# An attention and feed-forward kernel: where the units of one batch are scored, in which order a hand-written list puts them between the matmuls, and how the last block is cut

## The chip, the core and the metric

The kernel runs on one core of a Trainium2 chip. The metric is the device time of one execution in microseconds. A core has TensorE (matmuls), VectorE, ScalarE and GpSimd, which work side by side, each on its own queue in order, and a SyncE queue (SP) that only issues transfers. Engines wait for one another by semaphores.

## What is computed

Two steps follow each other. The first is attention over 8 batches of 576 positions with 8 heads of 64. Heads 0 to 3 see the 32 last positions ("plain"), heads 4 to 7 see every fourth of the last 128 ("dilated"). The second is a gated feed-forward block on the 4608 tokens of 512 values that the attention gives.

```python
def _attn_ref(q, k, v):
    B, H, S, D = q.shape                      # 8, 8, 576, 64
    scores = 1.0 / np.sqrt(D) * np.matmul(q, k.transpose(0, 1, 3, 2))
    rel = pos[:, None] - pos[None, :]
    mask_plain = (rel >= 0) & (rel < 32)
    mask_dil = (rel >= 0) & (rel < 128) & (rel % 4 == 0)
...
    attn = np.exp(scores - np.max(scores, axis=-1, keepdims=True))
    attn = attn / (np.sum(attn, axis=-1, keepdims=True) + 1e-09)
    return np.matmul(attn, v)

def _moe_ref(x, w_gate, w_val, w_out):        # x: 4608 x 512
    g = x @ w_gate                            # 512 x 1536
    gelu = 0.5 * g * (1.0 + erf(g * inv_sqrt2))
    return gelu * (x @ w_val) @ w_out         # 1536 x 512
```

## The kernel before, in words

**The feed-forward block** sets the frame. The tokens are cut into nine chunks of 512 (`run_chunk`, line 904). Each chunk c has two stages. In *gate stage* c, 96 matmuls of 128x512 (`ffn1_part`, line 636) make twelve blocks of the gate and of the value, four matmuls each; ScalarE applies the GELU to a gate block (`g0` to `g11`, line 801), VectorE multiplies with the value block (`u0` to `u11`, line 806). In *output stage* c, 48 matmuls of 128x512 (`ffn2`, line 643), twelve for each of four token blocks, multiply with w_out; ScalarE copies each block out of PSUM and SP stores it (`e0@c` to `e3@c`, `store`, lines 651 to 658). The store of the fourth block of a stage falls into the gate stage after it. The last token block of chunk 8 goes through `last_block` (line 660): its 512 columns are taken as two halves of twelve matmuls each, ScalarE copies the first (line 678) and SP stores it, VectorE copies the second (line 676) and ScalarE's queue stores it.

**The attention** is cut into 32 units of two heads of one batch: unit n is of batch n // 4. In batches 2 and 3 the dilated pairs come first, in the others the plain ones. A unit has these pieces, each a short word of the lists below:

- `Sn`: scores on TensorE (`two_s`, line 473); `Pn`: exponential on ScalarE (line 508); `Mn`: mask multiplied on VectorE (line 513).
- `Dn`: sums over the keys, on TensorE (`two_den`); `Nn`: products with v, on TensorE (`two_num`).
- the reciprocals of the sums, in one of two ways: `Tn` and `Bn` on VectorE (a transpose, line 597, a reciprocal, line 599, and a transpose back, line 614), or `An` on ScalarE (a logarithm, line 606, and an exponential, line 608).
- `Xn`: the product of both, written by VectorE into `xT` (line 627), the operand of the gate stages. `pair` (line 357) tells which of the four 128-row parts of `xT` a unit fills.

The number behind an @ is a place in PSUM: for S a bank (a unit takes two), for D and N 0 for banks 4 and 5, or 1 for banks 6 and 7. Two words with a plus between them are *joint*: their 64x64 matmuls are put into different quarters of TensorE's array alternately (`emit_tiles`, line 448, matmuls on line 457). A word alone is issued as 128x128 matmuls (`emit`, line 446).

**The loads.** `Fb` (`load_first`, line 291) loads q and k of batch b through SP into a staging tile, and GpSimd casts them to 16 bits (lines 221 and 233). `Hb` (`load_rest`, line 317) has SP turn them (four transposing transfers, line 273), loads v, and has GpSimd spread k into blocks for the scores (lines 289 and 281) and cast v (line 262). `R` is H3, F4 and H4. The staging tile, the 16-bit tile and the turned k (`dense`) are each there once, so a batch's loads wait for the casts and spreads of the batch before.

**The order** is written out by hand (`tc.manual_schedule()`, line 55). For each stage there is a list of words, `gates[c]` (line 829) or `outs[c]` (line 865), which `run_program` (line 782) takes one after the other: a number emits so many matmuls of the stage, any other word emits its piece at that place, each into the queue of its engine. `E` and `G` load ScalarE's function table for the attention and for the GELU. `firsts[c]` (line 893) gives the order of the first 16 matmuls of a gate stage as triples: block, gate or value, and the part of `xT` that is read, so that parts which come late are read late. The gate blocks use banks 0 to 3 in turn (`gate_banks`, line 753), the output blocks the pair of banks that `out_banks` (line 779) gives. Output stage c usually carries the four units of batch c + 1; their last N and X stand in the gate stage after it. Before the change, output stage 3 carries batch 4 and also S20, S21, P20, P21 and D20 of batch 5, whose loads F5 and H5 stand in gate stage 3.

Of the kernel before, what the change touches and what calls it, by code (L numbers as in the profile page):

```python
# [21 lines left out]
def kernel(  # L22
# [12 lines left out]
    NT, DM = out.shape  # L35
# [624 lines left out]
    def last_block(c, tb, bank):  # L660

        osb = osbp.tile([P, DM], F32, tag="osb")
        t0 = c * CH + tb * P
        for half in range(2):
            cs = slice(half * DM // 2, (half + 1) * DM // 2)
            for fc in range(NNB):
                nc.tensor.matmul(  # L667
                    ps[:, bank + 2 * half - 2, cs],
                    u_all[:, fc, tb * P : (tb + 1) * P],
                    wo_t[fc // 4][:, fc % 4, cs],  # L670
                    start=(fc == 0),
                    stop=(fc == NNB - 1),
                )
            src = ps[:, bank + 2 * half - 2, cs]
            if half:
                nc.vector.tensor_scalar(osb[:, cs], src, 1.0 / USCALE, None, ALU.mult)
            else:
                nc.scalar.activation(osb[:, cs], src, AF.Copy, bias=0.0, scale=1.0 / USCALE)
            (nc.scalar if half else nc.sync).dma_start(out=out[t0 : t0 + P, cs], in_=osb[:, cs])
# [102 lines left out]
    def run_program(c, words, mms, banks):  # L782
# [3 lines left out]
        for word in words.split():  # L786
# [10 lines left out]
            elif kind in units:  # L797
                units[kind](*args)
            elif kind == "g":
                g = ffn.tile([P, CH], F16, tag="g")  # L800
                nc.scalar.activation(g, ps[:, gate_banks(c, args[0])[0], :], AF.Gelu)  # L801
                tiles["g", args[0]] = g
            elif kind == "u":
                nb = args[0]
                val = ps[:, gate_banks(c, nb)[1], :]
                nc.vector.scalar_tensor_tensor(u_all[:, nb, :], tiles.pop(("g", nb)), USCALE, val, ALU.mult, ALU.mult)  # L806
            elif kind in "ew":
                at = args[1] if len(args) > 1 else c
                store(at, args[0], out_banks(at)[args[0]], "act" if kind == "e" else "dve")
            elif kind == "L":  # L810
                mms.clear()
                last_block(c, 3, banks[3])
            elif kind == "V":
                second_v() if args else second()
            elif kind == "F":
                load_first(args[0])
            elif kind == "H":
                load_rest(args[0])
            elif kind == "R":
                load_rest(3)  # L820
                load_first(4)
                load_rest(4)
            elif kind == "E":
                nc.scalar.preload_act_table_set("natural_log_exp_and_others")
            else:
                nc.scalar.preload_act_table_set("gelu_and_others")
# [7 lines left out]
            "t9@5@1 t11@7@0 5 g8 u8 8 g9 u9 8 g10 u10 1 t12@4@1 t14@6@0 t13@5@1 t15@7@0 7 g11 u11"  # L834
        ),
        1: (
            "4 N7@0 e3@0 F3 1 X7 1 G 8 g0 2 g1 1 u0 2 u1 2 g2 4 u2 4 g3 4 u3 4 g4 4 u4 4 g5 4 u5 4 g6 4 u6 4 g7 4 "
            "u7 4 g8 4 u8 4 g9 4 u9 4 g10 4 u10 4 g11 3"
        ),
        2: (  # L840
            "4 N11@0 e3@1 R 1 X11 G 7 g0 3 g1 u0 3 u1 3 g2 4 u2 4 g3 4 u3 4 g4 4 u4 4 g5 4 u5 4 g6 4 u6 4 g7 4 u7 "
            "4 g8 4 u8 4 g9 4 u9 4 g10 4 u10 4 g11 3"
        ),
        3: (
            "4 N15@0 e3@2 F5 H5 1 X15 G 7 g0 3 g1 u0 3 u1 3 g2 4 u2 4 g3 4 u3 4 g4 4 u4 4 g5 4 u5 4 g6 4 u6 4 g7 "
            "4 u7 4 g8 4 u8 4 g9 4 u9 4 g10 4 u10 4 g11 3"
        ),
        4: (
            "G 6 e3@3 F6 H6 T20 3 g0 2 N20@1+D21@0 u0 1 B20 1 g1 4 u1 3 X20 1 g2 4 u2 N21@1 1 T21 3 g3 3 B21 3 u3 "
            "2 g4 1 X21 4 u4 3 g5 4 u5 4 g6 4 u6 4 g7 4 u7 4 g8 4 u8 4 g9 4 u9 4 g10 4 u10 4 g11 3"  # L850
        ),
        5: (
            "G 5 B24 N24@1+D25@0 e3@4 F7 H7 g0 1 X24 4 u0 1 N25@1 T25 2 g1 3 B25 4 u1 1 g2 2 X25 3 u2 3 g3 4 u3 4 "
            "g4 4 u4 4 g5 4 u5 4 g6 4 u6 4 g7 4 u7 4 g8 4 u8 4 g9 4 u9 4 g10 4 u10 4 g11 3"
        ),
        6: (
            "G 2 T28 4 e3@5 1 N28@1+D29@0 B28 g0 2 u0 3 X28 1 g1 4 u1 N29@1 1 T29 3 g2 3 B29 3 u2 2 g3 1 X29 4 u3 "
            "3 g4 4 u4 4 g5 4 u5 4 g6 4 u6 4 g7 4 u7 4 g8 4 u8 4 g9 4 u9 4 g10 4 u10 4 g11 3"
        ),
        7: (  # L860
            "G 6 e3@6 2 g0 3 u0 2 g1 4 u1 4 g2 4 u2 4 g3 4 u3 4 g4 4 u4 4 g5 4 u5 4 g6 4 u6 4 g7 4 u7 4 g8 4 u8 4 "
# [2 lines left out]
    }  # L864
    outs = {
        0: (
            "V1 F2 S4@4+S5@6 1 E P4 10 P5 1 M4 S6@2+S7@6 M5 1 P6 2 D4@0 P7 1 M6 3 T4 2 e0@0 3 M7 1 e1@0 H2 2 B4 7 "
            "N4@1+D5@0 1 A5 X4 5 N5@0+D6@1 e2@0 1 A6 X5 5 N6@1+D7@0 1 A7 X6 1"
        ),
        1: (  # L870
            "1 u11 5 S8@0+S9@6 1 E P8 10 P9 M8 1 S10@0+S11@4 e0@1 M9 1 P10 2 D8@1 P11 1 M10 3 T8 e1@1 5 M11 "
            "N8@0+D9@1 B8 1 A9 3 X8 2 N9@1 e2@1 2 X9 2 D10@0 1 A10 5 N10@1+D11@0 1 A11 X10 1"
        ),
        2: (
            "1 u11 5 S12@2+S13@6 1 E P12 10 P13 M12 1 S14@2+S15@4 e0@2 M13 1 P14 2 D12@1 P15 1 M14 3 T12 e1@2 5 "
            "M15 N12@0+D13@1 B12 1 A13 3 X12 2 N13@1 e2@2 2 X13 2 D14@0 1 A14 5 N14@1+D15@0 1 A15 X14 1"
        ),
        3: (
            "1 u11 5 S16@0+S17@6 1 E P16 10 P17 1 M16 S18@0+S19@4 e0@3 M17 2 P18 1 D16@1 P19 1 M18 3 A16 M19 4 "
            "N16@0+D17@1 e1@3 S20@0 A17 X16 5 P20 N17@1+D18@0 1 A18 X17 1 S21@0 1 M20 2 P21 N18@0+D19@1 1 e2@3 "  # L880
            "X18 2 A19 4 M21 1 N19@1+D20@0 1 X19"
        ),
        4: (
            "1 u11 5 S22@2+S23@4 1 E P22 10 P23 M22 1 S24@2+S25@6 e0@4 M23 1 P24 2 D22@0 P25 1 M24 3 A22 1 M25 3 "
            "N22@1+D23@0 e1@4 1 X22 6 T23 1 e2@4 4 B23 N23@1+D24@0 1 X23 6 T24"
        ),
        5: (
            "1 u11 5 S26@0+S27@4 1 E P26 10 P27 M26 1 S28@0+S29@6 e0@5 M27 1 P28 2 D26@0 P29 1 M28 1 S30@0 A26 1 "
            "M29 3 N26@1+D27@0 P30 1 X26 1 e1@5 1 S31@0 1 P31 1 T27 5 M30 e2@5 N27@1+D28@0 B27 4 M31 4 X27 3"
        ),  # L890
        6: "D30@0 u11 1 E A30 5 N30@1+D31@0 1 T31 5 X30 N31@0 e0@6 4 B31 4 X31 5 e1@6 12 e2@6 11",
    }
    firsts = {
        0: "000 100 002 102 001 101 010 110 012 112 011 111 003 103 013 113",
        1: "000 001 010 011 002 012 100 101 102 110 111 112 003 013 103 113",
        2: "002 003 012 013 000 010 102 103 100 112 001 011 101 113 110 111",
        3: "002 003 012 013 000 010 102 103 100 112 001 011 101 113 110 111",
        4: "000 001 002 010 011 012 100 003 013 101 102 103 110 111 112 113",
        5: "000 001 002 003 010 011 012 013 100 101 102 103 110 111 112 113",
        6: "000 001 002 003 010 011 012 013 100 101 102 103 110 111 112 113",  # L900
        7: "000 001 002 003 010 011 012 013 100 101 102 103 110 111 112 113",
    }

# [38 lines left out]
```

## Time and profile before

| what | us |
|---|---|
| median of six runs | 335.56 |
| lowest and highest of them | 333.42, 337.39 |
| the profiled execution's own time | 337.39 |
| its span, first to last instruction | 335.7 |
| TensorE busy | 325.9 |
| VectorE busy | 159.3 |
| ScalarE busy | 157.6 |
| GpSimd busy | 149.9 |

The mean granted clock of TensorE is 0.995. The profiled execution is one of the six. Its span is what the profile's views divide; 1.7 us of its time lie outside. Starts of the stages in that execution, read off the order of the matmuls: gate stage 3 at 126, output stage 3 at 146.9, gate stage 4 at 166.3, output stage 4 at 188.2, gate stage 5 at 201.2, output stage 5 at 222.9. The last matmul ends at 332.45.

The profile has, beside busy times, the span in 40 slices (each 8.4 us, busy shares in tenths), a list of waits (who waited for whom, us in total, times, longest), the chain of work that ended last, and the instructions in order of time. A matmul of 512 columns shows a mean of 379 ns there since the matmuls are pipelined; from start to start it is 0.216 us. ACT stands for ScalarE, DVE for VectorE, PE for TensorE, PEld for its weight loads, POOL for GpSimd.

### The profile page before, as it was taken

Reading aid. Unit: us, or ns where it says so; the run is one execution under the profiler, and the core shown is the slowest. Engines: PE = TensorE matmul, PEld = TensorE weight load, DVE = VectorE, ACT = ScalarE, POOL = GpSimd, SP = SyncE. Lnnn points to the kernel's source line nnn. Section 1 sums busy time; section 2 is a strip of 40 time slices with the busy share of each in tenths; the row PEclk is TensorE's granted clock in tenths of the full one; section 3 lists DMA queues with packets and bytes.
Section 4 is the critical chain, followed back from the end, with each engine's and each line's share of the span. In section 5 each row is a group of like instructions: output and inputs, shape, how many; then the busy total and the mean of one; then the engine's idle time right before and its main releaser. Section 6 shows DMA issues by size and latency. Waiting matters only on the chain.

```text
span 335.7 us, 7368 instructions
## 1 busy us (share of the span) xinstructions
PE 325.9 (97%) x2959; PEld 160.9 (48%) x2959; DVE 159.3 (47%) x241; ACT 157.6 (47%) x236; POOL 149.9 (45%) x246
## 2 busy tenths in 40 slices
PE   7899999999999999996999999999999999999996
PEld 5744545444544454443544454445444544444443
DVE  6854654434643364432584478347743424303320
ACT  2763567436653566366733563357335343223321
POOL 8899777649437748444925841484000000000000
PEclk9999999999999999999899999999999999999999
DMA  8999986898798998999779636973100110020002
GB/s 185 195 195 180 197 171 148 231 175 213 172 265 184 195 231 159 252 199 173 192 181 240 158 113 151 245 174 94 62 2 1 65 62 0 2 94 31 0 33 94
DMA packets 109026, 47.97 MB, mean 143 GB/s; under 512 B 83648, under 2 KB 104512, under 8 KB 108992
## 3 DMA queue, kind: packets, MB, share of 16 engines
q1 hardware_dynamic: 97216, 39.99, 51.9%
q0 software_dynamic: 11216, 6.79, 14.2%
q10 hardware_dynamic: 560, 0.72, 0.8%
q8 instruction: 23, 0.38, 0.4%
q14 instruction: 11, 0.09, 0.1%
HBM read 37.75 MB, written 9.44 MB: 141 GB/s over the span
## 4 chain that ended last, share of the span: by engine, by line
PE 86%; DMA 7%; SPq 3%; POOL 1%; DVE 1%; issue 1%; ACT 0%; DVEq 0%; POOLq 0%
PE ps L636 52%; PE ps L643 26%; PE ps L457 4%; PE ps L446 3%; DMA dense<-s 2%; DMA wg<-in_moe_w_gate_dram 2%; DMA xT<-in_q_dram 2%; SPq L214 1%; DMA stage<-in_q_dram 1%; PE ps L667 1%; SPq L217 1%; POOL q L289 1%; PE ps L387 1%; POOL xT L176 0%; SPq L658 0%
## 5 line engine op out<-in xcount | busy, mean ns | idle before, releaser
L806 DVE SCALAR_TENSOR_TENSOR u_all<-g,ps 128x512 f16<-128x512 f16 x108 | 73.8, 687 | 104.7 <-PE ps L636 101.3
L801 ACT ACTIVATE g<-ps 128x512 f16<-128x512 f32 x108 | 64.1, 597 | 112.2 <-PE ps L636 112.2
L636 PE MATMUL ps<-xT,wg 128*128 128x512 f16 x432 | 113.8, 379 | 0.4 <-DMA wg<-in_moe_w_gate_dram 0.2
L636 PE MATMUL ps<-xT,wv 128*128 128x512 f16 x432 | 112.8, 379 | 0.0
L643 PE MATMUL ps<-wo,u_all 128*128 128x512 f16 x420 | 100.1, 382 | 0.0
L636 PEld LDWEIGHTS <-wv 128*128 128x128 f16 x432 | 42.2, 98 | 50.0
L636 PEld LDWEIGHTS <-wg 128*128 128x128 f16 x432 | 42.0, 98 | 49.9 <-issue 0.8
L643 PEld LDWEIGHTS <-u_all 128*128 128x128 f16 x420 | 37.9, 98 | 40.8 <-issue 0.3
L262 POOL CAST v<-stage 64x576 f16<-64x576 f32 x60 | 43.4, 723 | 6.5 <-DMA stage<-in_v_dram 3.4
L627 DVE TENSOR_TENSOR xT<-ps,rb 128x576 f16<-128x576 f32 x32 | 29.9, 937 | 22.2 <-PE ps L457 16.1
L221 POOL CAST s<-stage 128x640 f16<-128x640 f32 x24 | 17.1, 741 | 38.4 <-DMA stage<-in_q_dram 24.8
L508 ACT ACTIVATE P<-ps 128x832 f16<-128x832 f32 (+1 forms) x32 | 25.5, 834 | 15.6 <-PE ps L457 10.6
L654 ACT ACTIVATE osb<-ps 128x512 f32<-128x512 f32 x34 | 20.2, 595 | 26.0 <-PE ps L643 25.7
L289 POOL COPY q<-dense 64x1152 f16<-64x1152 f16 (+1 forms) x28 | 20.2, 720 | 15.5 <-DMA dense<-s 11.9
L281 POOL COPY q<-dense 64x512 f16<-64x512 f16 x28 | 16.4, 612 | 6.7 <-DMA dense<-s 3.7
L233 POOL CAST s<-stage 128x512 f16<-128x512 f32 x24 | 14.1, 617 | 10.1 <-DMA stage<-in_q_dram 5.2
L606 ACT ACTIVATE lg<-ps 128x576 f32<-128x576 f32 x18 | 11.7, 652 | 10.2 <-PE ps L457 6.8
L513 DVE TENSOR_TENSOR P<-P,two_d 128x768 f16<-128x768 f16 x14 | 10.1, 736 | 11.0 <-ACT P L508 10.7
L513 DVE TENSOR_TENSOR P<-P,two_p 128x832 f16<-128x832 f16 x14 | 10.1, 734 | 9.7 <-ACT P L508 9.6
L457 PEld LDWEIGHTS <-v 64*64 64x64 f16 x380 | 9.1, 110 | 8.5 <-issue 6.8
L608 ACT ACTIVATE rb<-lg 128x576 f32<-128x576 f32 x18 | 12.3, 683 | 0.6
L597 DVE STREAM_TRANSPOSE dt<-ps 128x576 f32<-128x576 f32 x14 | 10.8, 774 | 1.7 <-ACT rb L608 1.7
(81 smaller groups left out, 197.7 us busy)
## 6 DMA issues: line engine op xcount, KB each, us to landing
out_dram<-osb SPq DMA_DIRECT2D x35, 256.0 KB, 2.3
stage<-in_v_dram SPq DMA_DIRECT2D x32, 144.0 KB, 3.6
stage<-in_v_dram SPq DMA_DIRECT2D x28, 128.0 KB, 3.2
stage<-in_q_dram SPq DMA_DIRECT2D x24, 128.0 KB, 3.5
stage<-in_k_dram SPq DMA_DIRECT2D x24, 128.0 KB, 2.9
stage<-in_q_dram SPq DMA_DIRECT2D x6, 512.0 KB, 4.5
stage<-in_k_dram SPq DMA_DIRECT2D x6, 512.0 KB, 5.5
wg<-in_moe_w_gate_dram POOLq DMA_DIRECT2D x6, 256.0 KB, 6.8
```

The lines of the kernel that those rows point to most:

```text
L221: nc.gpsimd.tensor_copy(s16[:, 1280 * t + 640 * g : 1280 * t + 640 * g + 640].rearrange("p (k c) -> p k c", k=5), st_of(i).rearrange("p (k ...
L262: nc.gpsimd.tensor_copy(dst[half_of(x), at, half_of(x, g * swap)], st[half_of(x), at])
L289: nc.gpsimd.tensor_copy(out_, src[half].rearrange("p g (j c) -> p g j c", c=64))
L457: nc.tensor.matmul(o[cols], lhs[rows, cols], rhs[rows], start=st, stop=end, skip_group_check=True)
L508: nc.scalar.activation(pt[:, 0 : src.shape[1]], src, AF.Exp, bias=0.0, scale=scale)
L513: nc.vector.tensor_tensor(pt, pt, mask, ALU.mult)
L627: nc.vector.tensor_tensor(dst, num, rb, ALU.mult)
L636: nc.tensor.matmul(ps[:, bank, :], w[:, kc, ns], xT[kc][:, tok], start=first, stop=end)
L643: nc.tensor.matmul(ps[:, bank, :], u_all[:, fc, tb * P : (tb + 1) * P], wo_t[fc // 4][:, fc % 4, :], start=(fc == 0), stop=(fc == NNB - 1),)
L654: nc.scalar.activation(osb, ps[:, bank, :], AF.Copy, bias=0.0, scale=1.0 / USCALE)
L801: nc.scalar.activation(g, ps[:, gate_banks(c, args[0])[0], :], AF.Gelu)
L806: nc.vector.scalar_tensor_tensor(u_all[:, nb, :], tiles.pop(("g", nb)), USCALE, val, ALU.mult, ALU.mult)
```

## The change

Three things are altered. `last_block` cuts the last token block into 384 and 128 columns instead of 256 and 256. No unit of batch 5 is in output stage 3 any more; S20 and S21 are the first joint words of output stage 4, which now carries all of batch 5 and, as words alone, S24 and S25 of batch 6. And the lists of the stages 1 to 6 (in stage 0 one matmul's place at the end) are drawn anew: single words N9 and D10, and N13 and D14, become joint; the reciprocals of units 8, 12, 20, 21 and 23 are made by A instead of T and B; places in PSUM, the places of stores and of the units that are left over into a gate stage, and the orders in `firsts` are altered with them. The order of SP's and GpSimd's queues is the same but for the width of the last store.

```diff
--- before.py
+++ after.py
@@ -662,7 +662,7 @@
         osb = osbp.tile([P, DM], F32, tag="osb")
         t0 = c * CH + tb * P
         for half in range(2):
-            cs = slice(half * DM // 2, (half + 1) * DM // 2)
+            cs = slice(384 * half, 384 + 128 * half)
             for fc in range(NNB):
                 nc.tensor.matmul(
                     ps[:, bank + 2 * half - 2, cs],
@@ -834,28 +834,29 @@
             "t9@5@1 t11@7@0 5 g8 u8 8 g9 u9 8 g10 u10 1 t12@4@1 t14@6@0 t13@5@1 t15@7@0 7 g11 u11"
         ),
         1: (
-            "4 N7@0 e3@0 F3 1 X7 1 G 8 g0 2 g1 1 u0 2 u1 2 g2 4 u2 4 g3 4 u3 4 g4 4 u4 4 g5 4 u5 4 g6 4 u6 4 g7 4 "
+            "5 N7@0 e3@0 F3 1 X7 1 G 7 g0 2 g1 1 u0 2 u1 2 g2 4 u2 4 g3 4 u3 4 g4 4 u4 4 g5 4 u5 4 g6 4 u6 4 g7 4 "
             "u7 4 g8 4 u8 4 g9 4 u9 4 g10 4 u10 4 g11 3"
         ),
         2: (
-            "4 N11@0 e3@1 R 1 X11 G 7 g0 3 g1 u0 3 u1 3 g2 4 u2 4 g3 4 u3 4 g4 4 u4 4 g5 4 u5 4 g6 4 u6 4 g7 4 u7 "
+            "5 N11@1 e3@1 R 1 X11 G 7 g0 3 g1 u0 3 u1 2 g2 4 u2 4 g3 4 u3 4 g4 4 u4 4 g5 4 u5 4 g6 4 u6 4 g7 4 u7 "
             "4 g8 4 u8 4 g9 4 u9 4 g10 4 u10 4 g11 3"
         ),
         3: (
-            "4 N15@0 e3@2 F5 H5 1 X15 G 7 g0 3 g1 u0 3 u1 3 g2 4 u2 4 g3 4 u3 4 g4 4 u4 4 g5 4 u5 4 g6 4 u6 4 g7 "
+            "5 N15@0 e3@2 F5 H5 1 X15 G 7 g0 3 g1 u0 3 u1 2 g2 4 u2 4 g3 4 u3 4 g4 4 u4 4 g5 4 u5 4 g6 4 u6 4 g7 "
             "4 u7 4 g8 4 u8 4 g9 4 u9 4 g10 4 u10 4 g11 3"
         ),
         4: (
-            "G 6 e3@3 F6 H6 T20 3 g0 2 N20@1+D21@0 u0 1 B20 1 g1 4 u1 3 X20 1 g2 4 u2 N21@1 1 T21 3 g3 3 B21 3 u3 "
-            "2 g4 1 X21 4 u4 3 g5 4 u5 4 g6 4 u6 4 g7 4 u7 4 g8 4 u8 4 g9 4 u9 4 g10 4 u10 4 g11 3"
+            "2 N19@1 e3@3 F6 H6 1 X19 1 G 8 g0 3 g1 u0 3 u1 3 g2 4 u2 4 g3 4 u3 4 g4 4 u4 4 g5 4 u5 4 g6 4 u6 4 "
+            "g7 4 u7 4 g8 4 u8 4 g9 4 u9 4 g10 4 u10 4 g11 3"
         ),
         5: (
-            "G 5 B24 N24@1+D25@0 e3@4 F7 H7 g0 1 X24 4 u0 1 N25@1 T25 2 g1 3 B25 4 u1 1 g2 2 X25 3 u2 3 g3 4 u3 4 "
-            "g4 4 u4 4 g5 4 u5 4 g6 4 u6 4 g7 4 u7 4 g8 4 u8 4 g9 4 u9 4 g10 4 u10 4 g11 3"
+            "G 2 N23@1+D24@0 1 e3@4 F7 H7 X23 6 T24 3 g0 2 N24@1+D25@0 g1 u0 1 B24 4 u1 2 g2 1 X24 3 u2 2 N25@1 "
+            "T25 2 g3 3 B25 3 u3 2 g4 1 X25 4 u4 3 g5 4 u5 4 g6 4 u6 4 g7 4 u7 4 g8 4 u8 4 g9 4 u9 4 g10 4 u10 4 "
+            "g11 3"
         ),
         6: (
-            "G 2 T28 4 e3@5 1 N28@1+D29@0 B28 g0 2 u0 3 X28 1 g1 4 u1 N29@1 1 T29 3 g2 3 B29 3 u2 2 g3 1 X29 4 u3 "
-            "3 g4 4 u4 4 g5 4 u5 4 g6 4 u6 4 g7 4 u7 4 g8 4 u8 4 g9 4 u9 4 g10 4 u10 4 g11 3"
+            "G 4 T28 2 e3@5 2 g0 2 N28@1+D29@0 u0 1 B28 2 g1 2 T29 5 u1 N29@0 g2 1 X28 3 B29 4 u2 1 g3 2 X29 4 u3 "
+            "2 g4 4 u4 4 g5 4 u5 4 g6 4 u6 4 g7 4 u7 4 g8 4 u8 4 g9 4 u9 4 g10 4 u10 4 g11 3"
         ),
         7: (
             "G 6 e3@6 2 g0 3 u0 2 g1 4 u1 4 g2 4 u2 4 g3 4 u3 4 g4 4 u4 4 g5 4 u5 4 g6 4 u6 4 g7 4 u7 4 g8 4 u8 4 "
@@ -864,40 +865,40 @@
     }
     outs = {
         0: (
-            "V1 F2 S4@4+S5@6 1 E P4 10 P5 1 M4 S6@2+S7@6 M5 1 P6 2 D4@0 P7 1 M6 3 T4 2 e0@0 3 M7 1 e1@0 H2 2 B4 7 "
-            "N4@1+D5@0 1 A5 X4 5 N5@0+D6@1 e2@0 1 A6 X5 5 N6@1+D7@0 1 A7 X6 1"
+            "V1 F2 S4@4+S5@6 1 E P4 10 P5 1 M4 S6@2+S7@6 M5 1 P6 2 D4@0 P7 1 M6 3 T4 2 e0@0 3 M7 1 e1@0 H2 2 B4 8 "
+            "N4@1+D5@0 1 A5 X4 5 N5@0+D6@1 e2@0 1 A6 X5 5 N6@1+D7@0 1 A7 X6"
         ),
         1: (
-            "1 u11 5 S8@0+S9@6 1 E P8 10 P9 M8 1 S10@0+S11@4 e0@1 M9 1 P10 2 D8@1 P11 1 M10 3 T8 e1@1 5 M11 "
-            "N8@0+D9@1 B8 1 A9 3 X8 2 N9@1 e2@1 2 X9 2 D10@0 1 A10 5 N10@1+D11@0 1 A11 X10 1"
+            "1 u11 5 S8@0+S9@6 1 E P8 10 P9 M8 1 S10@0+S11@4 e0@1 M9 1 P10 2 D8@1 P11 1 M10 3 A8 1 M11 3 "
+            "N8@0+D9@1 e1@1 1 A9 X8 7 e2@1 1 N9@1+D10@0 1 A10 X9 8 N10@0+D11@1 1 A11 X10"
         ),
         2: (
-            "1 u11 5 S12@2+S13@6 1 E P12 10 P13 M12 1 S14@2+S15@4 e0@2 M13 1 P14 2 D12@1 P15 1 M14 3 T12 e1@2 5 "
-            "M15 N12@0+D13@1 B12 1 A13 3 X12 2 N13@1 e2@2 2 X13 2 D14@0 1 A14 5 N14@1+D15@0 1 A15 X14 1"
+            "1 u11 5 S12@2+S13@4 1 E P12 10 P13 M12 1 S14@2+S15@6 e0@2 M13 1 P14 2 D12@0 P15 1 M14 3 A12 1 M15 3 "
+            "N12@1+D13@0 e1@2 1 A13 X12 7 e2@2 1 N13@0+D14@1 1 A14 X13 8 N14@1+D15@0 1 A15 X14"
         ),
         3: (
-            "1 u11 5 S16@0+S17@6 1 E P16 10 P17 1 M16 S18@0+S19@4 e0@3 M17 2 P18 1 D16@1 P19 1 M18 3 A16 M19 4 "
-            "N16@0+D17@1 e1@3 S20@0 A17 X16 5 P20 N17@1+D18@0 1 A18 X17 1 S21@0 1 M20 2 P21 N18@0+D19@1 1 e2@3 "
-            "X18 2 A19 4 M21 1 N19@1+D20@0 1 X19"
+            "1 u11 5 S16@0+S17@6 1 E P16 10 P17 1 M16 1 S18@0+S19@4 e0@3 M17 1 P18 1 D16@1 1 P19 1 M18 2 A16 1 "
+            "M19 4 N16@0+D17@1 e1@3 1 A17 X16 6 e2@3 N17@1+D18@0 1 A18 X17 6 N18@0+D19@1 1 A19 X18 3"
         ),
         4: (
-            "1 u11 5 S22@2+S23@4 1 E P22 10 P23 M22 1 S24@2+S25@6 e0@4 M23 1 P24 2 D22@0 P25 1 M24 3 A22 1 M25 3 "
-            "N22@1+D23@0 e1@4 1 X22 6 T23 1 e2@4 4 B23 N23@1+D24@0 1 X23 6 T24"
+            "1 u11 5 S20@2+S21@4 1 E P20 10 P21 1 M20 1 S22@2+S23@6 e0@4 M21 1 P22 1 D20@0 1 P23 1 M22 2 A20 "
+            "S24@2 M23 3 N20@1+D21@0 e1@4 P24 1 X20 3 A21 1 M24 S25@2 1 N21@1+D22@0 P25 1 X21 1 A22 3 M25 2 "
+            "N22@0+D23@1 e2@4 1 A23 X22 6"
         ),
         5: (
-            "1 u11 5 S26@0+S27@4 1 E P26 10 P27 M26 1 S28@0+S29@6 e0@5 M27 1 P28 2 D26@0 P29 1 M28 1 S30@0 A26 1 "
-            "M29 3 N26@1+D27@0 P30 1 X26 1 e1@5 1 S31@0 1 P31 1 T27 5 M30 e2@5 N27@1+D28@0 B27 4 M31 4 X27 3"
-        ),
-        6: "D30@0 u11 1 E A30 5 N30@1+D31@0 1 T31 5 X30 N31@0 e0@6 4 B31 4 X31 5 e1@6 12 e2@6 11",
+            "1 u11 5 S26@0+S27@4 1 E P26 10 P27 M26 2 S28@0+S29@6 e0@5 M27 1 P28 1 D26@0 1 P29 1 M28 1 S30@0 A26 "
+            "1 M29 4 N26@1+D27@0 P30 1 e1@5 X26 2 S31@0 1 P31 1 T27 3 e2@5 2 M30 1 N27@1+D28@0 B27 3 M31 4 X27 1"
+        ),
+        6: "D30@1 u11 1 E A30 6 N30@0+D31@1 1 T31 5 X30 e0@6 1 N31@1 3 B31 4 X31 4 e1@6 12 e2@6 11",
     }
     firsts = {
         0: "000 100 002 102 001 101 010 110 012 112 011 111 003 103 013 113",
-        1: "000 001 010 011 002 012 100 101 102 110 111 112 003 013 103 113",
-        2: "002 003 012 013 000 010 102 103 100 112 001 011 101 113 110 111",
-        3: "002 003 012 013 000 010 102 103 100 112 001 011 101 113 110 111",
-        4: "000 001 002 010 011 012 100 003 013 101 102 103 110 111 112 113",
-        5: "000 001 002 003 010 011 012 013 100 101 102 103 110 111 112 113",
-        6: "000 001 002 003 010 011 012 013 100 101 102 103 110 111 112 113",
+        1: "000 001 010 011 100 002 012 101 102 110 111 112 003 013 103 113",
+        2: "002 003 012 013 102 000 010 103 100 112 113 001 011 101 110 111",
+        3: "002 003 012 013 102 000 010 103 100 112 113 001 011 101 110 111",
+        4: "000 001 002 010 011 012 100 101 102 110 003 013 103 111 112 113",
+        5: "000 001 002 010 011 012 100 101 102 110 003 013 103 111 112 113",
+        6: "000 001 002 010 011 003 012 013 100 101 102 103 110 111 112 113",
         7: "000 001 002 003 010 011 012 013 100 101 102 103 110 111 112 113",
     }
```

## The prediction

> **What bounds the kernel now.** First the page: the row of busy times, and the two rows of the span in 40 slices that show TensorE and its clock.
>
> ```profile
> PE 325.9 (97%) x2959; PEld 160.9 (48%) x2959; DVE 159.3 (47%) x241; ACT 157.6 (47%) x236; POOL 149.9 (45%) x246
> PE   7899999999999999996999999999999999999996
> PEclk9999999999999999999899999999999999999999
> ```
>
> TensorE sets the time; the others are under half. After the start only one slice of 8.4 us is open, the 19th (151 to 159 us: a 6), and the clock dips once, one slice later (an 8). Next the list of waits: of TensorE's own, only one is long.
>
> ```profile
> PEld L446 <- POOL q L289: 2.9, 1, 2.9
> PE ps L446 <- POOL q L289: 2.7, 1, 2.7
> ```
>
> The line 446 emits one unit alone, the line 289 is GpSimd's spread of the plain k blocks. The chain that ended last shows what came before it:
>
> ```profile
> 143.95 4.12 DMA stage<-in_q_dram
> 148.07 7.50 DMA dense<-s
> 155.70 1.15 POOL q L289
> 156.90 1.16 POOL q L289
> 158.10 0.54 PE ps L446 x9
> 158.64 1.58 PE ps L643 x5
> ```
>
> At 158.10 TensorE starts S20, the first scores of batch 5. It had been empty since 155.33 (2.75 us); it waited for a transfer that turns batch 5's k and for the spread behind it. Behind the stall five 128x512 matmuls take 1.58 us where a few stages on twelve take 2.70. So I asked for busy time and clock in half-microsecond stretches (the columns: us, TensorE, its weight loads, VectorE, ScalarE, GpSimd, clock, DMA share, GB/s):
>
> ```profile
> 158.50:159.00 0.50, 0.50 (x7) 0.26 (x5) 0.00 (x0) 0.32 (x1) 0.08 (x1) 1.00 0.14 37
> 159.00:159.50 0.50, 0.50 (x3) 0.16 (x2) 0.00 (x0) 0.50 (x1) 0.50 (x2) 0.58 0.75 223
> 162.00:162.50 0.50, 0.50 (x10) 0.50 (x8) 0.50 (x1) 0.48 (x1) 0.50 (x2) 0.51 0.79 178
> 162.50:163.00 0.50, 0.50 (x7) 0.22 (x4) 0.09 (x1) 0.28 (x1) 0.50 (x1) 1.00 0.88 202
> ```
>
> Between these rows the clock stands at 0.50 throughout, from about 159.1 to 162.5: 3.4 us at half speed, a loss of 1.7 us. The stall thus costs 2.75 + 1.7 = 4.45 us. A cross-check: output stage 3 lasts 146.9 to 166.3 = 19.4 us; its parts (48 matmuls at 0.216, two joint S at 0.59, four joint N and D at 0.6, three single units at 0.34) make 15.0. The rest is 4.4.
>
> **The change part by part.**
>
> *S20 and S21 leave output stage 3.* The only wait on GpSimd goes: -2.75 us. Does the clock loss go with it? The row: idle 2.75 us, then 3.4 us at 0.50. The rule: the Trainium skill, "TensorE: Matmul & The Clock Gate", Part 1, has the clock halved after at least one idle window of about 3.4 us, its practical table warns of gaps above some 3 us, and the windows run freely. By the rule a gap of 2.75 us need not cost anything, and the gain would be 2.75; by the row it is 4.45. The measurement decides for this execution: -1.70. But a free-running window means other executions of the kernel before may escape the loss, and I come back to that.
>
> The work itself is not less: before, S24 with S25 was joint and S20, S21 single; now S20 with S21 is joint and S24, S25 single. Twelve joint S segments stand in both instruction lists: 0. What waits for the moved units: their exponentials (ScalarE) and masks (VectorE), which also move to stage 4. No load moves against another one: the queues of SP and GpSimd have the same order in both programs but for the last store's width.
>
> *What is late next.* All later work arrives 4.45 us earlier, so the next deadlines count. Batch 6: its plain k was spread at 186.3 and used at 192.6, 6.3 us to spare; now S24 stands 2.4 us later in the stage (19 matmuls and a joint S ahead of it become 23, two joint S and a D), and its loads, which wait on stage 3's last store and on the v casts ending at 168.4, come at least 3 us earlier. Spare: about 7. Batch 7: spread 221.2, used at 227.4, 6.2 to spare; its loads are released by stage 4's last store, which now sits behind one more normalization (below), 0.9 us later: 5.3 to spare. Neither bites.
>
> *T and B become A in stages 1 to 4* (units 8, 12, 20, 21, 23). VectorE loses five times 0.774 + 0.267 + 0.773 = 9.1 us, ScalarE gains five times 0.652 + 0.683 = 6.7 us, all beside the matmuls if ScalarE keeps up. In stages 1 and 2 it was idle for 1.2 us ahead of its next piece. In stage 4 it is loaded as never before; before, that stage ran thus:
>
> ```profile
> 193.15 1.62 ACT L508 ACTIVATE P<-ps 128x832 f16<-128x832 f32 x2 [1.11 <-PE ps L457]
> 194.66 0.66 ACT L606 ACTIVATE lg<-ps 128x576 f32<-128x576 f32 x1
> 195.34 0.68 ACT L608 ACTIVATE rb<-lg 128x576 f32<-128x576 f32 x1
> 195.94 0.58 ACT L654 ACTIVATE osb<-ps 128x512 f32<-128x512 f32 x1
> ```
>
> Start to start that is 0.70 to 0.76 for a P, 0.68 + 0.60 = 1.28 for an A, and 0.5 for a store when the next piece is ready (163.48 to 163.97 in stage 3). From P22 on (5.23 us after the stage's start, as P18's group had it in stage 3) the queue holds, in order, P22, P23, A20, a store, P24, A21, P25, A22, a store, A23, the table load (1.28) and the last store: 1.40 + 1.28 + 0.49 + 0.76 + 1.28 + 0.76 + 1.28 + 0.49 + 1.28 + 1.28 + 0.60 = 10.9, so it ends at 16.1. TensorE asks for that last bank at the tenth gate matmul: 14.44 (stage end) + 0.43 + 0.61 + 1.5 = 17.0. Inside the stage N21 with D22 comes at 10.2 and needs A21's logarithm (9.8); N22 with D23 comes at 12.3 and needs A22's (11.9). So the cover is 0.35 us at the tightest. With mean durations in place of start to start it is gone, and two waits of 0.1 appear. Behind a waiting N pair stand the matmuls of the stage, and behind them the next gate. Bounds: 0 to +0.6; I take +0.1, nearer to the measured spacing.
>
> *N9 with D10 and N13 with D14 become joint.* In stage 1 they stand alone at 0.35 and 0.36, hardly a trace behind them; a joint one takes 0.49 and slows what follows it (three matmuls in 0.75 us instead of 0.65): 0.59 against about 0.72. Twice -0.12: -0.25. Other N and D: as many joint and single as before.
>
> *Places shifted by one or two matmuls* (N7, N11, X19, the stores, the orders of the first 16 gate matmuls): work of the same kind in the same queues; TensorE shows no wait there today, and N19 in gate stage 4 keeps the pattern of N15 in gate stage 3, which runs without one: 0, bounds -0.1 to +0.4.
>
> *Last block as 384 and 128.* Now:
>
> ```profile
> 329.65 2.78 PE L667 MATMUL ps<-wo,u_all 128*128 128x256 f16 x24
> 331.16 0.38 ACT L678 ACTIVATE osb<-ps 128x256 f32<-128x256 f32 x1 [0.71 <-PE ps L667]
> 332.47 0.42 DVE L676 TENSOR_SCALAR osb<-ps 128x256 f32<-128x256 f32 x1 [9.63 <-PE ps L667]
> 332.93 0.38 ACTq L679 DMA_DIRECT2D out_dram<-osb x1
> ```
>
> The matmuls keep their columns in sum: 2.63 us. The end is set by VectorE's copy (0.42; at 512 columns 0.69, so 0.285 at 128) and its store: -0.13, and a little for a smaller store. The first part's store is issued at 332.3 instead of 331.57 and lands between 1.7 (128 KB) and 2.0 us (256 KB) later, near 334.2; the second lands near 334.5: the second still ends it. The row for narrow matmuls: S units of 96 columns with own weights run nine in 0.34 us, 38 ns each, so 128 columns at some 55 ns. The rule: the same page, Back-to-back issue gap, gives 81 ns for a stream of weight loads with 128-column matmuls; twelve times 26 ns would be +0.3 us. The trace already shows faster ones. I take -0.15, bounds -0.25 to +0.2.
>
> **Sum**, against the profiled execution (337.39, span 335.7, 1.7 outside): -2.75 - 1.70 - 0.25 - 0.15 + 0.1 = -4.75, so 332.6, span 331.0. That execution is the slowest of the six (333.42 to 337.39, median 335.56). TensorE waits nowhere else after 17.6 us, so what differs from run to run is either the stall, clock loss included, or the start. If it is the stall, every run comes to about 332.6, and the fastest, only 0.8 above that, had nearly none; if it is the start, the median falls by the whole sum, to 330.8. The first is more natural (a chain of transfers against a fixed deadline, with a clock loss that comes or doesn't), but the slowest run will have had a somewhat slow start too: of the 1.83 us above the median I give it 0.3. Predicted: 332.3, -1.0% of the median.
>
> **Rivals.**
> 1. *The stall is in every run; the start varies.* For it: the start hangs on transfers up to 17.6 us. Against: the fastest run. 330.8.
> 2. *ScalarE becomes the bound in stage 4,* or one of the shifted places waits: PE idle before N21, N22 or the next gate, 0.6 to 2 us in all, too short to lower the clock. For: a cover of 0.35. Against: the sum of its queue. 333.0 to 334.3, say 333.7.
> 3. *Slower: a new stall in output stage 5.* Batch 7's loads come late for S28 with S29 (at present 6.2 us to spare). It costs more than it saves once they are later by the spare 5.3 plus 3.1, since 3.1 + 1.7 of clock equal the 4.75. For: batch 5's loads took 22 us to the spread, batch 7's 19, so such chains vary by 3. Against: 8 would be needed. From there on 337 and more.
> 4. *The change doesn't remove the stall.* Excluded as to S20; that GpSimd's k merely makes another one wait would show in the list of waits, and the spare times speak against it; in rival 3.
>
> **How the numbers follow.** Likeliest 0.65 (331.3 to 333.3), rival 1 0.13, rival 2 0.15, rival 3 0.07. About 1% (3.4 us) is what a measurement of this kernel can tell from no change; it lies at 332.2, inside the likeliest case. Of that case I put half below: 0.32, with rival 1 0.45 faster. Within 1%: 0.33 + 0.15 = 0.48. Slower: 0.07. The range leaves out rival 3 and the outer ends: 330.6 to 334.4.
>
> **What would show it.** No wait of TensorE on line 289; its clock at 1.00 after the start; output stage 3 at about 14 us, stage 4 at 14.4; 31 more matmuls; VectorE busy about 9 us less, ScalarE about 7 more; the end after the last matmul 3.1 instead of 3.25 us. Wrong would be: waits of N pairs on ScalarE in stage 4, a dip of the clock anywhere else, GpSimd's spread of batch 7 ahead of S28, or a median that falls by much less or more than 3.3 us while the trace shows all that.

## The result, and the profile after

| | before | after |
|---|---|---|
| median, us | 335.05 | 332.75 |
| lowest to highest, us | 333.27 to 337.64 (39 runs) | 331.89 to 333.69 (18 runs) |
| profiled execution, us | 337.39 | 332.33 |
| its span, us | 335.7 | 330.6 |

The ratio is 0.9923 (95% interval 0.9905 to 0.9942): 0.8% faster, 2.3 us. Before's spread of 4.4 us has shrunk to 1.8 us; the upper end fell by 3.95 us, the lower by 1.4. The two profiled executions stand 5.06 us apart, more than the medians: the one of before took 2.3 us more than its kernel's median, and had the stall at its longest in any profile here. The intervals, here and below, leave out runs more than 1.5% above their kernel's fastest (one of 22 with the tail alone, five of 22 with the joint words of stages 1 and 2 alone), while medians and extremes are of all runs.

The granted clock averaged over a run tells whether a half-clock stretch like the one of the profiled execution was in it: 1.7 us lost of 335.7 make 0.995. Of 71 timed runs of the kernel before that stand beside the experiments below, seven have 0.995 or less; of the 18 of the changed kernel one has (its longest, 333.69 us; it was not profiled, so where its loss lies is open). So a median run of the kernel before had no such loss, and the fall of the median is waiting time and work, hardly clock.

The page after: TensorE and its clock in 40 slices, with the busy times.

```profile
PE 323.7 (98%) x2990; PEld 159.0 (48%) x2990; DVE 151.0 (46%) x226; ACT 163.0 (49%) x246; POOL 151.3 (46%) x246
PE   6999999999999999999999999999999999999996
PEclk9999999999999999999999999999999999999999
```

The open slice and the dip of the clock behind it are gone. VectorE is down by 8.3 us, ScalarE up by 5.4 (9 and 7 were predicted), and there are 31 more matmuls. In the list of waits of TensorE after its start, these are all the entries of 0.2 us and more for its matmuls (the others of the list lie within the first 15 us), and none of them is on GpSimd:

```profile
PE ps L643 <- DMA wo<-in_moe_w_out_dram: 0.2, 1, 0.2
PE ps L636 <- DVE xT L627: 0.2, 1, 0.2
PE ps L636 <- DMA wg<-in_moe_w_gate_dram: 0.2, 1, 0.2
```

The chain that ended last (start, us, what), at the place where batch 5 is now scored, output stage 4:

```profile
181.59 1.29 PE ps L643 x6
182.89 0.49 PE ps L457 x36
```

S20 with S21 is the joint piece of 36 matmuls at 182.89. In this execution the spread of batch 5's plain k ended at 155.92, so it has 27 us to spare where before it was 2.75 us late. Of the last instructions:

```profile
324.86 2.78 PE L667 MATMUL ps<-wo,u_all 128*128 128x384 f16 x24
327.69 0.29 DVE L676 TENSOR_SCALAR osb<-ps 128x128 f32<-128x128 f32 x1 [9.63 <-PE ps L667]
328.01 0.37 ACTq L679 DMA_DIRECT2D out_dram<-osb x1
```

VectorE's copy takes 0.29 us instead of 0.42; the matmuls still take 2.63 us in the chain.

**Where the 5.06 us of these two executions came from**, by the place of the same pieces in both chains. At gate stage 1 (59.8) they are level; the start of the changed one was 0.35 us earlier, but that was gone by then. At the end of output stage 2 the changed one leads by 0.24 us (125.70 against 125.94). At output stage 5 it leads by 4.60 (218.34 against 222.94), so stages 3 and 4 gave 4.36. In output stage 6 another 0.19 comes (its cause is further below), and the end behind the last matmul gives 0.25: 0.24 + 4.36 + 0.19 + 0.25 = 5.04, which is the difference of the spans (335.66 and 330.63).

### The profile page after: what moved, and what is told of

The parts are those of the page before. It is cut to its first block, busy times and chain, and to the rows that moved or that the text cites. A ratio compares the mean times of both kernels' runs of the same rounds, so it can differ in the third digit from the quotient of the medians.

```text
span 330.6 us, 7440 instructions
## 1 busy us (share of the span) xinstructions
PE 323.7 (98%) x2990; PEld 159.0 (48%) x2990; DVE 151.0 (46%) x226; ACT 163.0 (49%) x246; POOL 151.3 (46%) x246
## 4 chain that ended last, share of the span: by engine, by line
PE 86%; DMA 8%; POOL 3%; DVE 1%; issue 1%; POOLq 0%; DVEq 0%
PE ps L636 51%; PE ps L643 27%; PE ps L457 5%; DMA wo<-in_moe_w_out_dram 5%; DMA wg<-in_moe_w_gate_dram 2%; PE ps L446 2%; DMA xT<-in_q_dram 2%; POOL xT L176 1%; PE ps L667 1%; POOL v L206 1%; POOL wo L156 0%; POOL s L731 0%; DVE xT L627 0%; POOL wv L153 0%; POOL wg L153 0%
## 5 line engine op out<-in xcount | busy, mean ns | idle before, releaser
L636 PE MATMUL ps<-xT,wg 128*128 128x512 f16 x432 | 115.0, 379 | 0.3 <-DVE xT L627 0.2
L262 POOL CAST v<-stage 64x576 f16<-64x576 f32 x60 | 42.3, 705 | 8.5 <-DMA stage<-in_v_dram 5.5
L281 POOL COPY q<-dense 64x512 f16<-64x512 f16 x28 | 17.2, 640 | 4.8 <-DMA dense<-s 3.5
L606 ACT ACTIVATE lg<-ps 128x576 f32<-128x576 f32 x23 | 15.0, 652 | 7.6 <-PE ps L457 7.2
L608 ACT ACTIVATE rb<-lg 128x576 f32<-128x576 f32 x23 | 15.7, 684 | 0.7
L513 DVE TENSOR_TENSOR P<-P,two_p 128x832 f16<-128x832 f16 x14 | 10.8, 774 | 10.9 <-ACT P L508 10.8
L457 PE MATMUL ps<-P,v 64*64 64x96 f16 (+5 forms) x420 | 11.7, 199 | 0.0
```

Of the source, the lines that this page charges most:

```text
L262: nc.gpsimd.tensor_copy(dst[half_of(x), at, half_of(x, g * swap)], st[half_of(x), at])
L457: nc.tensor.matmul(o[cols], lhs[rows, cols], rhs[rows], start=st, stop=end, skip_group_check=True)
L513: nc.vector.tensor_tensor(pt, pt, mask, ALU.mult)
L636: nc.tensor.matmul(ps[:, bank, :], w[:, kc, ns], xT[kc][:, tok], start=first, stop=end)
```

## Experiments

The kernel before was run again beside them: median 334.67 us (332.99 to 337.54, 44 runs) with the first four, 335.00 us (333.71 to 337.07, 27 runs) with the next ones. The ratios are to these runs; they are not the quotients of the medians.

**The move alone.** The kernel before, with only four lists and two orders of the changed one:

```diff
-gates[4], gates[5], outs[3], outs[4], firsts[4], firsts[5] of the kernel before
+the same six of the changed kernel
```

> The kernel before with only the lists of output stages 3 and 4 and gate stages 4 and 5 of the changed kernel: no unit of batch 5 in output stage 3, units 20, 21 and 23 by A. Theory (the stall and the clock loss behind it are the gain): no wait of TensorE on GpSimd, clock 1.00 in all runs, 333.1 us, ratio 0.994, and the spread of the runs shrinks from 4 to under 2 us. Rival (the gain comes from the joint words, the lists of stages 1 and 2 and the tail): ratio 0.998 or more.

Measured: 333.25 us (333.01 to 334.80, 7 runs), ratio 0.9927 (0.9901 to 0.9954). The list of waits has none of TensorE's matmuls on GpSimd, the clock row shows nines only, and all seven runs have a mean clock of 0.999 or 1.00. The wait goes with the move: most of the gain of the whole change is here (1.4 us by the medians, beside 334.67), and the spread shrinks with it (six of the seven runs within 0.4 us; the seventh is 334.80). The rest of the changed kernel's 2.3 us is about what its other parts measure in the profiles below: 0.28 for the joint words, 0.19 for output stage 6, 0.25 for the tail, 0.7 in all.

**The tail alone.**

```diff
-            cs = slice(half * DM // 2, (half + 1) * DM // 2)
+            cs = slice(384 * half, 384 + 128 * half)
```

> The kernel before with only the last block as 384 and 128 columns. Theory: the end after the last matmul 0.14 us shorter, ratio 0.9996, not to be told from 1 by the times; the stall is still there, so the runs spread over 4 us as before, and those with a clock of 1.00 are the shorter ones by 1.7 us or more. Rival by the back-to-back rule: twelve 128-column matmuls take 0.97 us instead of 0.67 and the end comes 0.15 us later.

Measured: 334.72 us (332.98 to 338.05, 22 runs), ratio 0.9993 (0.9972 to 1.0014), not to be told from 1. The profile shows the piece by itself: from the start of VectorE's copy, which follows the last matmul in the chain, to the end of the span (to the nanosecond in the traces) there are 2.94 us here and 2.94 to 2.95 in the three other kernels with this cut, against 3.19 in all four with two halves. The difference is 0.25 us; the matmuls are 2.63 us with either cut, so the dear 128-column matmul of the rule (the expectation's is that of the Trainium skill, "TensorE: Matmul & The Clock Gate", Back-to-back issue gap, which the prediction cites) didn't come. The single clocks fit the expectation in the main: four of the 22 runs have a mean clock of 0.995, and took 336.12 to 338.05 us; the eighteen at 0.999 or 1.00 took 332.98 to 336.34, with a median 2.6 us lower. But runs at full clock also spread by 3.4 us, so the clock is not all that differs between them; no profile of a long one at full clock was kept. The profiled execution shows that a stall need not lower the clock: the stall is there, and the clock doesn't drop. Its stretches of a microsecond (TensorE's busy time is the third number, the clock the third from the end):

```profile
155.00:156.00 1.00, 0.28 (x26) 0.17 (x16) 0.57 (x1) 0.84 (x2) 0.96 (x1) 1.00 1.26 274
156.00:157.00 1.00, 0.00 (x0) 0.00 (x0) 0.18 (x1) 0.79 (x2) 0.98 (x1) 1.00 0.59 187
157.00:158.00 1.00, 0.78 (x11) 0.58 (x12) 0.00 (x0) 0.20 (x1) 0.94 (x3) 1.00 0.70 209
158.00:159.00 1.00, 1.00 (x20) 0.43 (x22) 0.00 (x0) 0.66 (x1) 0.96 (x3) 1.00 0.42 119
```

The gap is 1.9 us by the list of waits, and the clock stays at 1.00 after it. Nothing in stage 3 was changed here: that is the kernel before's stall in another execution.

**The joint words of stages 1 and 2 alone, and the changed kernel without them.**

```diff
-gates[2], gates[3], outs[1], outs[2], firsts[2], firsts[3] of the kernel before
+the same six of the changed kernel          (and the reverse for the second)
```

> The kernel before with only the new lists of output stages 1 and 2 and gate stages 2 and 3 (N9 with D10 and N13 with D14 joint, units 8 and 12 by A). Theory: output stages 1 and 2 each 0.13 us shorter, but the stall at S20 is ended by batch 5's loads and takes back what is gained, since the loads start no earlier by as much: ratio 0.999 to 1.001. Rival (a joint word is worth its 0.13 us wherever it stands, or more): ratio 0.999 or less.

> The changed kernel with the old lists of output stages 1 and 2 and gate stages 2 and 3. Theory: no stall, so the 0.25 us of the two joint words is lost in full: 333.0 us, 0.25 above the changed kernel, ratio to the kernel before 0.993 to 0.994; the profile shows output stages 1 and 2 at 13.8 instead of 13.67 us each. Rival: the same as the changed kernel.

Measured: the first 334.75 us (332.69 to 339.60, 22 runs), ratio 0.9984 (0.9961 to 1.0008); the second 332.95 us (332.12 to 333.86, 6 runs), ratio 0.9919 (0.9888 to 0.9950). The times can't tell either from its neighbour: 0.25 us is below what they resolve, so the question whether a stall swallows a gain ahead of it stays open. Nor is it explained that eight of these 22 runs of the first have a mean clock of 0.995 or less, against four of 44 of the kernel before beside them. The stage lengths in the chains are plain: output stage 1 takes 13.67 us with the joint words (77.18 to 90.85) in the first, and 13.81 without (77.50 to 91.31) in the second. In the profiled execution of the first, though, the loads were in time. Its chain at S20, the nine matmuls on line 446:

```profile
154.53 0.51 PE ps L457 x23
155.03 0.48 PE ps L446 x9
155.51 1.08 PE ps L643 x5
```

S20 follows the N and D before it at once, the five matmuls behind it take 1.08 us and not 1.58, and this execution (332.74 us) is as short as the changed kernel's.

The end of batch 5's plain spread in four profiled executions: 158.05 (before), 157.16 (the tail alone), 154.70 (the joint words alone), 156.96 (the changed kernel without them). S20's turn in the kernel before came at 155.3. The order of SP's queue is the same in all (in the third the loads stand one matmul later in gate stage 3); the issue of the transposing transfer of k takes 4.00, 3.45, 2.53 and 3.82 us there. In the kernel before and the one with the tail alone, which are the same up to the last block, the ends still differ by 0.89 us. So the stall is a race against transfers whose length differs from execution to execution.

**S20 later in the same stage.** S20 five matmuls later, S21 two, P20 and P21 each one word further back, in the list of output stage 3 (the rest of the list is left out here):

```diff
-S20@0 A17 X16 5 P20 N17@1+D18@0 1 A18 X17 1 S21@0 1 M20 2 P21 N18@0+D19@1 1 e2@3
+A17 X16 5 S20@0 N17@1+D18@0 P20 1 A18 X17 3 S21@0 1 M20 N18@0+D19@1 P21 1 e2@3
```

> The kernel before with S20 five matmuls later in output stage 3 and S21 two matmuls later behind it, the rest of the list kept. Theory (the stall is a fixed deadline missed by 0 to 2.75 us, and only a long gap brings the clock loss): the gap is 1.1 us shorter, so 1.65 at most and often 0, the clock loss becomes rare, and the median falls to 333.4 to 334.0, ratio 0.996 to 0.998, without any unit leaving the stage. Rival (only taking batch 5 out of the stage removes the wait; S21 or P20 then waits instead): ratio 0.999 or more.

Measured: 334.20 us (332.98 to 336.57, 14 runs), ratio 0.9986 (0.9961 to 1.0012). In the profiled execution 0.5 us of the wait is left:

```profile
PE ps L446 <- POOL q L289: 0.5, 1, 0.5
```

The median expected was 333.4 to 334.0, so this is a miss by a little, and the interval holds both the theory's ratio and 1: inconclusive. Five of the fourteen runs are still above 335.4, four of them at a mean clock of 0.998 or 1.00. The trace shows a second deadline behind the first, which neither the theory nor its rival names: N20 with D21, in gate stage 4, starts at 165.16 but gets its next matmuls only at 165.49, when the last cast of v that N20 needs has ended (165.43). In the profiled execution of the joint words alone, without a wait at S20, N20 starts just as that cast ends (164.07). So S20 moved by a microsecond runs into the next word that waits for the same batch; moved by a stage, all words of batch 5 gain time (N20 comes at 189.48 in the changed kernel, 23 us after these casts). How much of the fourteen runs' spread is due to N20 was not measured.

**ScalarE's cover in output stage 4.** The changed kernel, the logarithm done twice for four units:

```diff
-        nc.scalar.activation(lg, psf[:, c0 : c0 + S], AF.Ln)
+        for _ in range(2 if 20 <= n < 24 else 1):
+            nc.scalar.activation(lg, psf[:, c0 : c0 + S], AF.Ln)
```

> The changed kernel with the logarithm of units 20 to 23 done twice on ScalarE (0.69 us more each, 2.76 in all, same result), all in output stage 4. Theory (ScalarE's cover in that stage is 0.35 us at the tightest and 0.9 at the gate): TensorE waits ahead of S25, of N21 with D22 and of N22 with D23 and the next gate, 2.0 to 2.5 us in all, in gaps of about 1 us that don't lower the clock: about 335 us. Rival (ScalarE is far from being the bound there): under 0.7 us.

Measured: 335.03 us (334.47 to 336.10, 12 runs), 2.3 us above the changed kernel; the whole gain is gone (ratio to before 1.0002, 0.9980 to 1.0024). TensorE waits in the four places named, in order of time (from line 606 on, this kernel's lines are numbered one higher):

```profile
192.11 0.53 PE L446 MATMUL ps<-q 128*128 128x96 f16 x9 [0.22 <-ACT P L508]
193.34 0.31 PE L457 MATMUL ps<-P,two_ones 64*64 64x288 f16 x2 [0.32 <-ACT lg L607]
196.02 0.23 PE L457 MATMUL ps<-P,v 64*64 64x96 f16 x2 [0.53 <-ACT lg L607]
201.07 0.38 PE L637 MATMUL ps<-xT,wv 128*128 128x512 f16 x1 [0.35 <-ACT osb L655]
```

The idle times sum to 1.4 us only. Idle is counted from the end shown for the last matmul, which for 512 columns lies 0.379 - 0.216 = 0.16 us behind the moment when the next could have started; four times that is an estimate of most of the rest. 2.76 us of added work became 2.3 us, so some 0.5 us were covered, between the 0.35 of the tightest word and the 0.9 at the gate.

**What a gap costs.** The changed kernel with artificial gaps in gate stages 7 and 8, where GpSimd is free: a matmul, a VectorE copy of it, a chain of GpSimd copies, and a matmul that reads the last. Work is added, none left out. Each of the four kernels was executed once. "The rule" in the expectations is the one that the prediction cites from the Trainium skill, "TensorE: Matmul & The Clock Gate", Part 1; the last two expectations were written when the first two runs were known.

```diff
+    def gap():
+        nc.tensor.matmul(ps[:, 6, 0:P], ones[:, 0:P], ones[:, 0:P], start=True, stop=True)
+        nc.vector.tensor_copy(gap_a[:, 0:P], ps[:, 6, 0:P])
+        nc.gpsimd.tensor_copy(gap_b[:, 0:P], gap_a[:, 0:P])
+        for _ in range(2):            # 3 and 1 in the others
+            nc.gpsimd.tensor_copy(gap_a[:, P:CH], gap_b[:, P:CH])
+            nc.gpsimd.tensor_copy(gap_b[:, 0:P], gap_a[:, 0:P])
+        nc.tensor.matmul(ps[:, 6, 0:P], gap_b[:, 0:P], ones[:, 0:P], start=True, stop=True)
```

> The changed kernel with six artificial gaps of TensorE in gate stages 7 and 8: a small matmul waits for a VectorE copy and a chain of five GpSimd copies behind the matmul before it; by the copies' rows each gap is about 2.4 us. It adds work and leaves none out. By the rule (the clock halves after an idle window of 3.4 us): no clock loss, +14 us in all. By the row of the kernel before (2.75 us brought a loss, while the kernel before with the tail changed shows none after 1.9): clock losses of 1.7 us behind some of the six, at a share of about 2.4/3.4 if the window runs freely and needs only to be mostly idle.

> The same with chains of seven GpSimd copies, about 3.2 us a gap. By the rule still no loss, or few; by the row of the kernel before a loss of 1.7 us behind most of the six.

> The changed kernel with the same six gaps as the run with 2.5 to 2.7 us, but a chain of three GpSimd copies: about 1.8 us a gap. With 2.5 to 2.7 us two of six gaps brought a clock loss of 1.6 us, with 3.2 to 3.4 us all six did. If a loss needs the free-running window to be mostly idle, none of six is lost here; if it is a matter of chance in proportion to the gap, one or two are.

> The changed kernel with five gaps of 2.5 to 2.7 us at other places of gate stages 7 and 8. Theory (the place of the gap in a window that runs freely decides): again some of the five bring a loss of about 1.7 us, one to three. Rival (the two of six were peculiar to their places): none or all.

The loss behind each gap is summed from the granted clock in quarters of a microsecond over the 8 us after it (a quarter at 0.50 loses 0.125 us):

| run | gaps, us idle | loss behind each, us |
|---|---|---|
| one round of copies | 1.8, 1.8, 1.9, 2.0, 2.0, 2.0 | five 0, one 1.71 |
| two rounds | 2.5, 2.5, 2.6, 2.7, 2.7, 2.7 | four 0, two 1.6 and 1.7 |
| two, at other places (five gaps) | 2.2, 2.5, 2.7, 2.7, 2.7 | three 0, two 1.6 and 1.7 |
| three rounds | 3.2, 3.2, 3.3, 3.4, 3.4, 3.4 | 1.4, 1.4, 1.7, 1.7, 1.7, 2.9 |

The spans (351.6 and 363.5 with two and three rounds, against 330.6) agree: 15.8 us of idle time, 3.25 of loss and an estimated 0.3 around each gap make 20.9 of 21.0; 20.0, 10.8 and the same make 32.6 of 32.9. So neither reading of the expectations is right alone: at 2.5 to 2.7 us the loss comes in four of ten gaps, it comes after one of seven of 1.8 to 2.2, and after all six of 3.2 to 3.4. The threshold of about 3.4 us of idle time, read as safety below it, is refuted.

**What decides.** The traces hold each change of the clock to the nanosecond, and they answer what the runs were too few to answer by counting. The times between two changes are 3.413, 6.827, 10.240, 34.133, 37.547, 153.600 and 266.240 us, for example: 1, 2, 3, 10, 11, 45 and 78 times 3.4133. So the clock changes on a grid of 3.41 us, and the grid is not tied to the program: the first rise to full clock comes between 4.4 and 7.4 us in these profiles. Cut at this grid, two gaps of 2.73 us in the run with two rounds look thus (TensorE's busy time is the third number, the clock the third from the end):

```profile
311.23:314.64 3.41, 0.90 (x5) 0.29 (x3) 0.89 (x2) 0.60 (x1) 1.50 (x5) 1.00 0.00 0
314.64:318.05 3.41, 3.19 (x9) 1.27 (x10) 0.00 (x0) 0.60 (x1) 0.16 (x1) 0.50 0.00 0
321.47:324.88 3.41, 2.14 (x11) 0.86 (x9) 1.58 (x3) 0.72 (x2) 0.27 (x2) 1.00 0.00 0
324.88:328.29 3.41, 1.96 (x10) 0.95 (x11) 0.00 (x0) 0.60 (x1) 1.39 (x5) 1.00 0.02 5
328.29:331.70 3.41, 3.41 (x17) 1.57 (x16) 1.38 (x2) 1.19 (x2) 0.00 (x0) 1.00 0.00 0
```

The first lies almost whole in one stretch of the grid (2.51 us idle there), and the next stretch is at half clock. The second is cut in two by the grid (1.27 and 1.45 us), and nothing follows. The longest idle time of a gap within one stretch of the grid:

| run | loss followed | no loss |
|---|---|---|
| one round | 2.04 | 1.08, 1.37, 1.71, 1.77, 1.82 |
| two rounds | 2.47, 2.51 | 1.33, 1.45, 1.60, 1.87 |
| two, at other places | 2.25, 2.53 | 1.44, 1.55, 1.56 |
| three rounds | 2.13, 2.18, 2.39, 2.39, 2.59, 2.74 | |
| kernel before; the tail alone | 2.43 | 1.75 |

All 25 gaps sort without exception: up to 1.87 us idle in one stretch no loss, from 2.04 us on a loss. The clock falls at the end of that stretch (from 1.04 us before the end of the gap to 1.28 behind it) and returns one stretch later; once it took two, where 1.03 us of the gap still lay in the slow stretch. That agrees with the Trainium skill, "TensorE: Matmul & The Clock Gate", Part 1, in that the windows run freely and last about 3.4 us; it does not agree that a whole window must be idle: 2.04 us of 3.41, 60%, were enough here.

## Why the prediction was right, point by point

**The stall and its clock loss.** Of the profiled execution 2.75 + 1.70 = 4.45 us were put on them; 4.36 came back. The move alone shows that the wait is most of the gain in the medians too (333.25 us). The choice between row and rule was right for this execution, and the reservation with it, that others may escape the loss: its gap had 2.43 us in one stretch of the clock's grid, that of the tail alone (1.9 us) had 1.75. It was rarer than the prediction had to assume: with seven losses in 71 runs, the profiled execution was an unlucky draw, and the 1.70 us have next to no part in the fall of the median.

**From the profiled execution to the median.** The sum gave 332.6; I moved it to 332.3, since I gave the longest of the six runs a late start. That step was wrong: the start of the profiled execution was 0.35 us later than the changed one's, but both were level at 59.8, and the changed kernel's profiled execution (332.33) lies below its median (332.75), not above. The unmoved sum was 0.15 from the median; what was predicted is off by 0.45. The fall of the median is 2.3 us where 3.3 were predicted: 0.3 of the miss is that term, 0.15 the sum itself, and 0.5 is that the median of the kernel before, 335.56 in six runs, is 335.05 in 39. Of the two readings of the spread the first held: the spread goes when the stall goes. What makes the longest runs at full clock long, the length of the wait or something else, no profile shows. Rival 1, a stall in every run, is out: the profiled execution of the joint words alone had no wait at S20, and the median fell by 2.3 and not by 4.75.

**What is late next: nothing.** Batch 6's plain spread ended at 182.6 and S24 came at 188.5: 5.9 us to spare, where I had some 7. The sum had all later work 4.45 us earlier, but output stage 4 starts 6.57 us earlier (181.59 for 188.16), since stage 3 gave up the work of batch 5 too. Batch 7's ended at 217.45 and S28 came at 223.0: 5.6, where I had 5.3. Rival 3 didn't come.

**ScalarE in stage 4.** It holds the queue as worked out; the rows after:

```profile
186.93 1.51 ACT L508 ACTIVATE P<-ps 128x768 f16<-128x768 f32 x2 [1.40 <-PE ps L457]
...
197.27 0.60 ACT L654 ACTIVATE osb<-ps 128x512 f32<-128x512 f32 x1
```

From P22 to the end of the store there is no gap in the queue: 186.93 to 197.87 is 10.9 us, the sum predicted. The stage took 14.45 us (predicted 14.44), no wait of TensorE is listed in it, and the +0.1 wasn't needed. Rival 2 didn't come, but the doubled logarithm shows how near it was. Its gaps were called too short to lower the clock; that held for the four waits there (up to 0.53 us), but a single gap of 2.0 us in the runs with artificial gaps did lower it.

**The joint words.** -0.25 predicted; output stage 1 went from 13.81 to 13.67 us, output stage 2 likewise: -0.28 in the chain.

**The shifted places.** Costed at 0; output stage 6 gained 0.19. Before, N30 with D31 came five matmuls after A30's place and took 0.67 us; after, six, and it takes 0.47. Both stages hold the same pieces. The cause is a short wait for A30's logarithm, which the list of waits doesn't show and the prediction missed: D31 uses D30's place in PSUM; before, that logarithm ends at 260.13 and D31's first matmul starts at 260.18, 0.21 us after N30's (259.97); after, it ends at 255.53, and both start at 255.60. All five profiles with the old list have the 0.67, all three with the new one the 0.47. So the prediction's sentence that TensorE waits nowhere else is not quite right.

**The tail.** -0.15 predicted, -0.25 measured, at the end of the bounds: the copy gave its 0.13, and the smaller store 0.11 (1.63 us from issue to landing for 64 KB, 1.74 for 128 KB).

## What to carry to other kernels

When one engine is busy nearly everywhere, look for its one open slice. A stretch of lowered clock behind it belongs to the profiled execution; before it is counted into the median, look how many runs have it (seven of 71 here). A place that waits for a chain of transfers is better moved by a whole stage than by a microsecond: such chains ended up to 3 us apart in the profiles here (154.70 to 158.05), and other words wait for the same batch right behind the first. The gain in the median is then smaller than in the execution that happened to be profiled, but the spread goes. Before work is moved onto another engine, add up that engine's queue in the one stage where it is fullest: its share over the whole span (ScalarE 49%) says nothing of the half microsecond that is left there.

## What the runs showed of the hardware that was not expected

Whether a gap on TensorE costs nothing more or another 1.4 to 1.7 us at half clock was decided, in all 25 gaps here, by where it falls on the clock's grid of 3.41 us: 2.04 us of idle time or more within one stretch lowered the clock for the next, 1.87 or less did not. So gaps of 2.0 to 2.7 us did both, and no gap under 2.0 us was followed by a loss. The loss begins up to 1.28 us after the matmuls have resumed, so it must be looked for behind the stall; once it lasted two stretches (2.9 us lost). The same loads in the same order on the same queue ended up to 3.35 us apart in four executions, of four kernels that differ little ahead of them.
